# Output products of a two-layer linear-attention kernel: rounded parts replaced by plain float32, cut in pieces

## The chip, the cores and the metric

The kernel runs on one core of a Trainium2 chip. The metric is the device time of one execution in microseconds, the median of several runs. The core's engines each have a queue of their own: TensorE (PE in the profile, its weight loads PEld), VectorE (DVE), ScalarE (ACT), GpSimd (POOL) and SyncE (SP, which issues the DMAs here).

## The reference

The input x has 2048 rows of 640 columns, in float32. Two layers, each an attention part and a dense part, with the same weights in both:

```python
x = x + _A_ref(_layernorm(x, axis=-1), A_wqkv, A_w_phi, A_wo)
x = x + _B_ref(_layernorm(x, axis=-1), B_w1, B_b1, B_w2)
x = x + _A_ref(_layernorm(x, axis=-1), A_wqkv, A_w_phi, A_wo)
x = x + _B_ref(_layernorm(x, axis=-1), B_w1, B_b1, B_w2)
```

`_A_ref` forms queries, keys and values (32 heads of 20), maps queries and keys by a small matrix per head, takes the softmax of the result and of its negative as features, and does linear attention: `kv` and `z` are sums over all rows, and each row's output is a quotient of two products. The part that matters here is its last product, `o.reshape(B, S, D) @ wo`: 2048 x 640 by 640 x 640. `_B_ref` is a dense layer to 1536 columns, Mish, and a dense layer back to 640.

## The kernel before

Rows are worked on in 8 blocks (`NB`) of 256, each of two row tiles of 128 (`BT`). The 640 columns are 5 groups of 128 (`KD`) as an operand that is summed over, and two halves of 320 (`HC`) as an output.

Products that must be exact to float32 are made from rounded parts (`F32R`): an operand a is split into a high part (a rounded copy) and a low part (a less the high part), and one product becomes three: high by high, high by low, low by high. `project_half` (L352) does this for one half of one row tile: 5 x 3 = 15 matmuls into one PSUM tile. Some other products use plain float32 operands: `average` (L584, its matmuls at L594), the sums over keys (L432), and the folding of the feature matrices into the weights (`fold_phi`, L239, L250).

Each layer has three stages.

- `attend_first` runs over the blocks and makes queries, keys and values, and sums `kv` and `z` over all rows. After block 1 it also calls `load_o_weights` (L211), which reads the five row groups of `wo` through `make_five` (L199): raw rows are fetched into spare tiles, ScalarE makes the high part and GpSimd the low part (`make_parts`, L152 to L155).
- `attend_second` (L574) runs over the blocks again. `average` makes the attention output of one row tile in rows. `Transposed` (L279) turns two such tiles: TensorE transposes them into PSUM (L294), ScalarE copies the high part out (L299, recorded at its helper's line, L122), VectorE subtracts for the low part (L300). `Rows.half` (L621) then makes one half of one row tile of the output product, adds it to x (L624) and takes statistics of the sum (L625). In each block there are four such halves: r0's two go to two `one_tile`s, r1's two to one `mm_tile`. In between, the averages of the next block and its transposes are issued. Meanwhile the weights of the dense part are fetched and split (`fetches`, `makes`).
- `dense` does the two dense layers over the blocks, its matmuls at L703 and L745.

The order of instructions on TensorE and SyncE is written out by hand in `attend_second` (`tc.manual_schedule`). Elsewhere, and on the other engines, a planner orders the work by simulated times (`tc.block(schedule_with_timeline_sim=True)`), save where the code says what an instruction is to follow.

Of the kernel before, what the change touches and what calls it, by code (L numbers as in the profile page):

```python
# [8 lines left out]
F32 = mybir.dt.float32  # L9
F32R = mybir.dt.float32r  # L10
AF = mybir.ActivationFunctionType
# [5 lines left out]
P = 128  # L17
S = 2048
D = 640
# [3 lines left out]
KD = D // P  # L23
KF = F // P
BT = 2
BLK = BT * P
# [3 lines left out]
HC = D // 2  # L30
# [18 lines left out]
def kernel(  # L49
# [13 lines left out]
    nc = tc.nc  # L63
# [47 lines left out]
    x1_d = dram.tile([S, D], F32, name="x1_d")  # L111
# [40 lines left out]
    def make_parts(w, raw, ordered=False):  # L152
        for st, cs in raw:
            (act if ordered else nc.scalar.activation)(w[0][:, cs], st, AF.Copy)
            nc.gpsimd.tensor_tensor(w[1][:, cs], st, w[0][:, cs].bitcast(F32), op=ALU.subtract)  # L155
# [11 lines left out]
    def r2_pair(j):  # L167
        if j >= 10:
            w = r2_wide(j)
            return w[:, 0], w[:, 1]  # L170
        return tuple(wts.tile([P, D], F32R, tag=f"r2{s}{j}", name=f"r2{s}{j}") for s in "hl")
# [24 lines left out]
                nc.sync.dma_start(wp_d[1, s, k], kv_ws[k][s][:, :FW].bitcast(F32))  # L196
                nc.sync.dma_start(wp_d[0, s, k], q_ws[k][s][:, :FW].bitcast(F32))

    def make_five(j, rows):  # L199

        spares = five_spares(j)
        raws = [fetch_rows(rows(k), [spares[k]()]) for k in range(3)]
        yield
        for k in range(5):
            w = r2_pair(j + k)
            make_parts(w, raws[k])
            if k in (0, 1):
                raws.append(fetch_rows(rows(3 + k), [spares[3 + k]()]))
            yield w

    def load_o_weights():  # L211
        return list(make_five(KD, lambda k: wo[k * P:(k + 1) * P, :]))[1:]

    def w2_pair(f):

# [63 lines left out]
    class Transposed:  # L279


        def __init__(self, rows=None, cols=None):
            self.rows, self.cols, self.hs, self.ls = rows, cols, [], []

        def step(self):
            c0 = len(self.hs)
            n = min(2, KD - c0)
            if self.rows is None:
                ps = self.cols[c0 // 2]
            else:  # L290
                ps = one_tile().rearrange("p (c s) -> p c s", c=2)
                for c in range(n):
                    for t in range(BT):
                        nc.tensor.transpose(ps[:, c, t * P:(t + 1) * P],  # L294
                                            self.rows[t][:, (c0 + c) * P:(c0 + c + 1) * P], ident)
            nb = 8 if n == 2 else 4
            hi = work.tile([P, n, BLK], F32R, tag=f"xt{n}", name="xth", bufs=nb)
            lo = work.tile([P, n, BLK], F32R, tag=f"xt{n}", name="xtl", bufs=nb)
            act(hi, ps[:, :n], AF.Copy)  # L299
            nc.vector.tensor_tensor(lo, ps[:, :n], hi.bitcast(F32), op=ALU.subtract)  # L300
            for c in range(n):
                self.hs.append(hi[:, c, :])
                self.ls.append(lo[:, c, :])
# [48 lines left out]
    def project_half(ps, xts, t, ws, col, c, ks=range(KD), w=HC):  # L352
        sl = slice(t * P, (t + 1) * P)
        cs = slice(col + c * w, col + (c + 1) * w)
        for k in ks:
            h, l, wh, wl = xts.hs[k], xts.ls[k], ws[k][0][:, cs], ws[k][1][:, cs]
            for n, (a, r) in enumerate(((h, wh), (h, wl), (l, wh))):
                nc.tensor.matmul(ps[:, :w], a[:, sl], r, start=(k == 0 and n == 0),  # L358
                                 stop=(k == KD - 1 and n == 2))

    def both(ps, w=HC):

# [208 lines left out]
                mask[:r, :w].unsqueeze(1).unsqueeze(3).to_broadcast([r, q, w, DH + 1]), op=ALU.mult)  # L571
        yield

    def attend_second(x_src, x_dst, acc, fetches, makes, fetch_next, begin_next):  # L574
        kva, o_ws, loaded, rest = acc
        rows = {}
        div = [None]

        def tail():

            with tc.issue_after(div[0]):
                next(rest, None)

        def average(b, t):  # L584

            phs = loaded[b]
            po = mm_tile()
            for g in range(G):
                n = 120 if g < 10 else 80
                w = GW if g < 10 else 42  # L590
                c, j = divmod(g, 8)
                for q in range(2):
                    s0 = t * P + 64 * q
                    nc.tensor.matmul(  # L594
                        po[64 * q:64 * q + 64, c, GW * j:GW * j + w], phs[g][:n, s0:s0 + 64],
                        kvb[:n, g, :w], start=True, stop=True)
            o = row_tile()
            den = work.tile([P, H], F32, tag="r", name="den", bufs=2)
            pv = [po[:, c, :(DH + 1) * n].rearrange("p (h d) -> p h d", d=DH + 1)
                  for c, n in ((0, 24), (1, 8))]  # L600
            hh = (slice(0, 24), slice(24, H))
            for c in range(2):
                nc.vector.tensor_scalar_add(den[:, hh[c]], pv[c][:, :, DH], DEN_EPS)
            nc.vector.reciprocal(den, den)
            for c in range(2):
                n = hh[c].stop - hh[c].start
                ins = nc.vector.tensor_tensor(o.rearrange("p (h d) -> p h d", d=DH)[:, hh[c]], pv[c][:, :, :DH],
                                        den[:, hh[c]].unsqueeze(2).to_broadcast([P, n, DH]), op=ALU.mult)
                div[0] = ins.ins
            rows.setdefault(b, []).append(o)  # L610
            if t == BT - 1:
                del loaded[b]

        class Rows:


            def __init__(self, b, t):
                self.t, self.xt, self.ps = t, xs[b], None
                self.bn = work.tile([P, 2, 6], F32, tag="bn", name="bn", bufs=2)

            def half(self, c, ps):  # L621
                project_half(ps, cur, self.t, o_ws, 0, c)
                part = self.xt[:, self.t, c * HC:(c + 1) * HC]
                nc.vector.tensor_tensor(part, ps[:, :HC], part, op=ALU.add)  # L624
                nc.vector.bn_stats(self.bn[:, c], part)  # L625

            def mean(self):
                mv = work.tile([P, 2], F32, tag="mv", name="mv", bufs=3)
                nc.vector.bn_aggr(mv, self.bn)
                return mv  # L630

        with tc.manual_schedule(engines={mybir.EngineType.PE, mybir.EngineType.SP}):
            kv = finish_kv(kva)
            next(kv)
            next(rest)
            next(kv)
            loaded[1] = load(1)
            xs = {0: fetch(x_src, 0)}
            fetches[0]()
            next(rest)  # L640
            next(kv)
            next(rest)
            average(0, 0)
            average(0, 1)
            loaded[2] = load(2)
            average(1, 0)
            cur = Transposed(rows.pop(0)).all()
            average(1, 1)
            loaded[3] = load(3)
            for b in range(NB):  # L650
                if b == NB - 1:
                    ahead.all()
                elif b:
                    average(b + 1, 0)
                r0, r1 = Rows(b, 0), Rows(b, 1)
                r0.half(0, one_tile())
                if 0 < b < NB - 1:
                    average(b + 1, 1)
                tail()
                if b + 1 < NB:  # L660
                    xs[b + 1] = fetch(x_src, b + 1)
                if 0 < b and b + 3 < NB:
                    loaded[b + 3] = load(b + 3)
                if b == NB - 3:
                    fetch_next()
                r0.half(1, one_tile())
                mv0 = r0.mean()
                if b == NB - 2:
                    ahead = begin_next()
                py = mm_tile()  # L670
                r1.half(0, py[:, 0])
                if b + 1 < NB:
                    nxt = Transposed(rows.pop(b + 1)).all()
                r1.half(1, py[:, 1])
                norm_scale(b, [mv0, r1.mean()])
                xt = xs.pop(b)
                nc.sync.dma_start(row_block(x_dst, b), xt)
                makes[b]()
                if b + 1 < NB:
                    fetches[b + 1]()  # L680
                tail()
                if b < NB - 1:
                    cur = nxt
            for _ in rest:
                pass
        return ahead
# [134 lines left out]
    with tc.block(schedule_with_timeline_sim=True):  # L821
        src, first = x, None
        for layer in range(LAYERS):
# [35 lines left out]
            def begin_dense():  # L859
                return normed(0, x1t[0])  # L860

            begun = attend_second(src, x1_d, acc, [lambda s=s: fetch_step(*s) for s in steps],
                                  [lambda s=s: make_step(*s) for s in steps], fetch_dense, begin_dense)
            first = dense(x1_d, dst, w1s, w2s, [x1t[0], begun, None], last)
            src = dst
# [38 lines left out]
```

## Time and profile before

| | |
|---|---|
| median of 3 runs | 1397.88 us (1397.22 to 1398.19) |
| the profiled execution | 1397.5 us |
| its span, first to last instruction | 1395.7 us |
| mean granted clock of TensorE | 0.996 |
| PE busy | 1364.8 us (98%) |
| DVE busy | 1080.8 us (77%) |
| ACT busy | 592.4 us (42%) |
| POOL busy | 466.4 us (33%) |
| `attend_second` of layer one, first average to last half | 268.6 to 373.3 us |
| `attend_second` of layer two, the same | 944.5 to 1048.8 us |

A row of a group in the profile reads: line, engine, operation, output tile <- input tiles, shapes, count, then busy time and mean duration of one in ns, then the engine's idle time before them and what ended it. A row in order of time reads: start in us, duration in us, engine, line and the same names. A row of a stretch has its limits and length, then the busy time and number of instructions of PE, PEld, DVE, ACT and POOL, the granted clock, the DMA engines' share and GB/s. Matmuls overlap and their ends are modelled, so what one costs in a row of them is read from start to start.

### The profile page before, as it was taken

The numbers are of one execution on the slowest core, as the hardware profiler recorded it, in microseconds if no ns is written. First come the engines' busy times: TensorE is split into PE (matmuls) and PEld (weight loads), VectorE is DVE, ScalarE is ACT, GpSimd is POOL, SyncE is SP. The second block draws the span as 40 slices with busy tenths as digits, with TensorE's granted clock in tenths as the row PEclk, the third lists the DMA queues.
The fourth block names the chain that finished last, engine by engine and source line by source line (L and its number), as shares of the span: only waits on it lengthen the run. The fifth ranks groups of instructions, "written<-read, shape, count | busy, mean of one in ns | idle before, by whom it ended". The sixth has DMA issues, their size and how long they took to land. (4 is left out here: it accounts for less than half of the span.)

```text
span 1395.7 us, 30855 instructions
## 1 busy us (share of the span) xinstructions
PE 1364.8 (98%) x12866; PEld 1344.2 (96%) x12866; DVE 1080.8 (77%) x1814; ACT 592.4 (42%) x1039; POOL 466.4 (33%) x346
## 2 busy tenths in 40 slices
PE   7999999999999999999999999999999999999998
PEld 7989999899999999999999999999999999999998
DVE  5798888686688877788759988878667766777775
ACT  4444443321355454454454334332134544444443
POOL 1454544243442221222234454543344211211112
PEclk9999999999999999999999999999999999999999
DMA  8533423779534433444374333358965212333200
GB/s 312 166 60 77 75 41 70 204 224 317 194 89 95 100 82 60 102 114 95 103 258 85 78 72 70 58 126 253 273 246 172 76 29 68 95 96 95 59 37 20
DMA packets 350277, 169.03 MB, mean 121 GB/s; under 512 B 287097, under 2 KB 323689, under 8 KB 350137
## 3 DMA queue, kind: packets, MB, share of 16 engines
q1 hardware_dynamic: 350137, 167.06, 44.4%
q8 instruction: 101, 1.65, 0.5%
q14 instruction: 39, 0.32, 0.1%
HBM read 104.43 MB, written 62.59 MB: 120 GB/s over the span
## 5 line engine op out<-in xcount | busy, mean ns | idle before, releaser
L745 PE MATMUL mm<-r2h,ol 128*128 128x320 f32 x1280 | 305.3, 310 | 1.4 <-ACT ol L728 0.8
L729 POOL TENSOR_TENSOR ol<-big,ol 128x512 fp32r<-128x512 f32 (+1 forms) x98 | 130.1, 1329 | 456.2 <-ACT ol L728 390.9
L703 PE MATMUL one<-xtl,r1h 128*128 128x256 f32 x960 | 268.6, 280 | 2.0 <-DVE xtl L300 2.0
L703 PE MATMUL one<-xth,r1l 128*128 128x256 f32 x960 | 268.0, 279 | 0.0
L703 PE MATMUL one<-xth,r1h 128*128 128x256 f32 x960 | 266.5, 279 | 0.0
L745 PEld LDWEIGHTS mm<-r2h,ol 128*128 128x128 f32 x1280 | 219.1, 188 | 2.7 <-POOL ol L729 1.5
L745 PE MATMUL mm<-r2l,ol 128*128 128x320 f32 x640 | 197.3, 309 | 0.0
L358 PE MATMUL mm<-r1h,xth 128*128 128x304 f32 (+1 forms) x600 | 187.5, 313 | 6.6 <-ACT r L122 6.6
L358 PE MATMUL mm<-r1h,xtl 128*128 128x304 f32 (+1 forms) x600 | 184.7, 308 | 1.0 <-DVE xtl L300 1.0
L358 PE MATMUL mm<-r1l,xth 128*128 128x304 f32 (+1 forms) x600 | 184.4, 307 | 0.0
L703 PEld LDWEIGHTS one<-xtl,r1h 128*128 128x128 f32 x960 | 180.4, 188 | 2.7 <-DVE xtl L300 2.5
L703 PEld LDWEIGHTS one<-xth,r1l 128*128 128x128 f32 x960 | 180.4, 188 | 0.0
L703 PEld LDWEIGHTS one<-xth,r1h 128*128 128x128 f32 x960 | 179.9, 188 | 0.0
L718 DVE TENSOR_SCALAR big<-big 128x512 f32<-128x512 f32 (+1 forms) x98 | 55.9, 571 | 113.6 <-ACT big L716 113.5
L358 PE MATMUL mm<-r2h,xth 128*128 128x304 f32 (+1 forms) x460 | 142.2, 309 | 0.0
L358 PE MATMUL mm<-r2h,xtl 128*128 128x304 f32 (+1 forms) x460 | 140.4, 305 | 0.0
L358 PE MATMUL mm<-r2l,xth 128*128 128x304 f32 (+1 forms) x460 | 140.3, 305 | 0.0
L716 ACT ACTIVATE big<-one,b1s 128x256 f32<-128x256 f32 x192 | 80.8, 469 | 96.2 <-PE one L703 95.6
L358 PEld LDWEIGHTS mm<-r1h,xth 128*128 128x128 f32 x600 | 113.8, 190 | 8.1 <-ACT r L122 7.0
L720 ACT ACTIVATE big<-big,two 128x512 f32<-128x512 f32 (+1 forms) x98 | 70.3, 717 | 118.8 <-DVE big L719 116.2
L745 PEld LDWEIGHTS mm<-r2l,ol 128*128 128x128 f32 x640 | 120.2, 188 | 0.0
L399 POOL TENSOR_TENSOR r<-r,r 128x1280 f32<-128x1280 f32 x32 | 77.0, 2406 | 124.1 <-DVE r L398 108.7
(131 smaller groups left out, 3031.9 us busy)
## 6 DMA issues: line engine op xcount, KB each, us to landing
e_d<-r SPq DMA_DIRECT2D x128, 160.0 KB, 4.0
big<-e_d SPq DMA_DIRECT2D x32, 640.0 KB, 5.9
x_d<-xt SPq DMA_DIRECT2D x23, 640.0 KB, 3.9
xt<-x_d SPq DMA_DIRECT2D x22, 640.0 KB, 4.6
n_d<-xn SPq DMA_DIRECT2D x176, 80.0 KB, 2.3
xt<-in_x SPq DMA_DIRECT2D x16, 640.0 KB, 5.5
xn<-x_d SPq DMA_DIRECT2D x28, 320.0 KB, 4.1
v<-n_d SPq DMA_DIRECT2D x30, 256.0 KB, 3.1
```

The lines of the kernel that those rows point to most:

```text
L358: nc.tensor.matmul(ps[:, :w], a[:, sl], r, start=(k == 0 and n == 0), stop=(k == KD - 1 and n == 2))
L399: nc.gpsimd.tensor_tensor(eg, eg, r.unsqueeze(2).to_broadcast([P, 2 * H, DH]), op=ALU.mult)
L703: nc.tensor.matmul(ph[:, j, :], l, r, start=(n == 0), stop=(n == 3 * KD - 1))
L716: exps[0] = nc.scalar.activation(part(ta, 0)[:, j - js.start], ph[:, j, :], AF.Exp, bias=b1s[:, 2 * pr + j:2 * pr + j + 1]).ins
L718: nc.vector.tensor_scalar_min(e, e, E_CAP)
L720: nc.scalar.activation(r, n, AF.Ln, bias=two)
L729: nc.gpsimd.tensor_tensor(al[:, js], n, ah[:, js].bitcast(F32), op=ALU.subtract)
L745: nc.tensor.matmul(pys[t][:, c, :HC], l[:, j, sl], r, start=(f == 0 and n == 0), stop=(f == KF - 1 and n == 2))
```

## The change

The output product of attention takes whole operands in plain float32. `make_five` gets a flag: with it, ScalarE copies the raw rows of `wo` into a plain float32 tile, and no low part is made (the low tile is still allotted). `Transposed` gets a flag: with it, ScalarE copies the turned rows to a plain float32 tile, and VectorE's subtraction is left out. `project_whole` does one matmul per group of 128 summed columns and per piece of the output; the pieces are given by `cuts`. In layer one, each half of 320 is cut into 108, 106 and 106 columns. In layer two, row tile 0 is cut into 160 and 160, and row tile 1 is not cut.

```diff
-    def make_five(j, rows):
+    def make_five(j, rows, whole=False):
...
         for k in range(5):
-            w = r2_pair(j + k)
-            make_parts(w, raws[k])
+            if whole:
+                w = tuple(wts.tile([P, D], F32, tag=f"r2{s}{j + k}", name=f"r2{s}{j + k}") for s in "hl")
+                for st, cs in raws[k]:
+                    nc.scalar.activation(w[0][:, cs], st, AF.Copy)
+            else:
+                w = r2_pair(j + k)
+                make_parts(w, raws[k])
...
     def load_o_weights():
-        return list(make_five(KD, lambda k: wo[k * P:(k + 1) * P, :]))[1:]
+        return list(make_five(KD, lambda k: wo[k * P:(k + 1) * P, :], True))[1:]
...
             nb = 8 if n == 2 else 4
+            if self.whole:
+                hi = work.tile([P, n, BLK], F32, tag=f"xt{n}", name="xtw", bufs=nb)
+                act(hi, ps[:, :n], AF.Copy)
+                for c in range(n):
+                    self.hs.append(hi[:, c, :])
+                return
...
+    def project_whole(ps, xw, t, ws, c, cuts):
+
+        sl = slice(t * P, (t + 1) * P)
+        for k in range(KD):
+            for n, (c0, c1) in enumerate(zip(cuts, cuts[1:])):
+                nc.tensor.matmul(ps[:, c0:c1], xw.hs[k][:, sl], ws[k][0][:, c * HC + c0:c * HC + c1],
+                                 start=(k == 0 and n == 0), stop=(k == KD - 1), skip_group_check=True)
...
             def half(self, c, ps):
-                project_half(ps, cur, self.t, o_ws, 0, c)
+                cuts = (0, 108, 214, 320) if layer == 0 else ((0, 160, 320), (0, 320))[self.t]
+                project_whole(ps, cur, self.t, o_ws, c, cuts)
...
-            cur = Transposed(rows.pop(0)).all()
+            cur = Transposed(rows.pop(0), whole=True).all()
...
-                    nxt = Transposed(rows.pop(b + 1)).all()
+                    nxt = Transposed(rows.pop(b + 1), whole=True).all()
```

The rows that the dense part turns first (`begin_next`) keep their two parts, and so do all other products.

More of the change, by code (lines that the diff above doesn't have):

```diff
@@ L279, with __init__ @@
     class Transposed:
-        def __init__(self, rows=None, cols=None):
+        def __init__(self, rows=None, cols=None, whole=False):
             self.rows, self.cols, self.hs, self.ls = rows, cols, [], []
+            self.whole = whole
         def step(self):
@@ L572, in finish_kv, with attend_second @@
         yield
-    def attend_second(x_src, x_dst, acc, fetches, makes, fetch_next, begin_next):
+    def attend_second(layer, x_src, x_dst, acc, fetches, makes, fetch_next, begin_next):
         kva, o_ws, loaded, rest = acc
@@ L860, in begin_dense @@
                 return normed(0, x1t[0])
-            begun = attend_second(src, x1_d, acc, [lambda s=s: fetch_step(*s) for s in steps],
+            begun = attend_second(layer, src, x1_d, acc, [lambda s=s: fetch_step(*s) for s in steps],
                                   [lambda s=s: make_step(*s) for s in steps], fetch_dense, begin_dense)
```

## The prediction

> **What bounds the kernel now.** I read the page's first two parts, then the waits, then the stretches in which the changed products run, then the order of instructions inside one block of such a stretch.
>
> ```profile
> span 1395.7 us, 30855 instructions
> PE 1364.8 (98%) x12866; PEld 1344.2 (96%) x12866; DVE 1080.8 (77%) x1814; ACT 592.4 (42%) x1039; POOL 466.4 (33%) x346
> PEclk9999999999999999999999999999999999999999
> 268.60:366.44 97.84, 97.17 (x1215) 93.66 (x1215) 73.80 (x194) 24.47 (x41) 35.82 (x33) 1.00 0.78 246
> 944.47:1041.96 97.49, 96.81 (x1216) 93.31 (x1215) 74.11 (x197) 24.59 (x41) 35.81 (x33) 1.00 0.79 253
> PE mm L594 <- PE mm L594: 0.4, 1, 0.4
> PE one L358 <- DVE xtl L300: 0.2, 1, 0.2
> ```
>
> TensorE is busy for 98% of the span, and each of its 12866 matmul records has its own weight load record. The two rows of stretches (PE, PEld, DVE, ACT and POOL busy, then clock, DMA share, GB/s) are the two passes through the second half of attention, one per layer: 97.84 and 97.49 us, in which PE is idle 0.67 and 0.68 us, at a full clock. The last two rows are all the waits of PE that are listed inside them, one from each: 0.4 us behind its own averages and 0.2 us for a low part. Nothing else is late there. So whatever the change adds to PE's instructions in these stretches should come out at the end of the kernel, and what it takes off VectorE and GpSimd should not.
>
> **The products as they are.** One half (128 rows by 320 columns) is 5 x 3 = 15 products of rounded float32 parts. In the order of time (start, duration):
>
> ```profile
> 276.47 0.31 PE L358 MATMUL one<-r2l,xth 128*128 128x320 f32 x1
> ...
> 282.78 0.31 PE L358 MATMUL mm<-r2h,xtl 128*128 128x320 f32 x1
> 282.93 1.25 PE L294 MATMUL one<-ident,xn 128*128 128x128 f32 x10
> 267.20 0.46 PE L358 MATMUL one<-r2l,xth 128*128 128x304 f32 x1
> ...
> 268.22 0.46 PE L358 MATMUL one<-r2h,xtl 128*128 128x304 f32 x1
> 266.80:268.50 1.70, 1.70 (x8) 1.50 (x6) 1.05 (x4) 0.00 (x0) 0.00 (x0) 0.50 1.03 412
> ```
>
> Between 276.47 and 282.78 lie 43 steps from record to record (three halves less two records): 6.31 / 43 = 146.7 ns each, so a half takes 15 x 146.7 = 2.20 us. The row after them is the transposes of the next block's rows, which a later part uses. The last two steps of time are a piece at half the granted clock (0.50 in the last row): four steps in 1.02 us, 255 ns for 304 columns, 0.839 ns a column, which at the full clock is 0.4195. So 320 columns stream in 134.2 ns, and a rounded product has a fixed 12.5 ns on top.
>
> **The products as they will be.** Each half is 5 plain float32 products, cut into pieces. Layer one: three pieces (108, 106, 106). Layer two: two of 160 for row tile 0, one of 320 for row tile 1. With 8 blocks, 2 row tiles and 2 halves a layer, that is 32 halves in thirds, 16 in two pieces, 16 whole. The kernel has plain float32 products already: the averages (L594), the sums of keys and values (L432) and the folding of the feature weights (L250).
>
> ```profile
> L594 PE MATMUL mm<-kvb,big 120*64 120x63 f32 x1280 | 44.5, 225 | 0.9 <-PE mm L594 0.9
> L594 PE MATMUL mm<-kvb,ol 80*64 80x42 f32 x128 | 8.7, 212 | 0.0
> L432 PE MATMUL one<-big,v 128*21 128x40 f32 x2048 | 26.8, 205 | 0.0
> L250 PE MATMUL one<-big,raw x40: 261/275/421, 16.0 to 40.7; 120*128 120x114 f32 x40
> L703 PE MATMUL one<-xth,r1l 128*128 128x256 f32 x960 | 268.0, 279 | 0.0
> L745 PE MATMUL mm<-r2l,ol 128*128 128x320 f32 x640 | 197.3, 309 | 0.0
> 36.74 0.82 PE L250 MATMUL mm<-big,raw 120*128 120x114 f32 x6
> 37.39 0.83 PE L250 MATMUL one<-big,raw 120*128 120x114 f32 x6
> 38.06 0.83 PE L250 MATMUL mm<-big,raw 120*128 120x114 f32 x6
> 38.73 1.28 PE L250 MATMUL one<-big,raw 120*128 120x114 f32 x10
> 39.94 0.41 PE L250 MATMUL one<-big,r 40*128 40x38 f32 x2
> ```
>
> First, **the count**. An average issues 22 products, and there are 32 averages: 704, where the rows have 1280 + 128 = 1408. The sums of keys are 32 x 32 = 1024 products and 2048 records. So a plain product is two records, each with its own weight load. A half becomes 5 x 3 x 2 = 30, 5 x 2 x 2 = 20 or 5 x 2 = 10 records, in place of 15.
>
> Second, **the columns**. The duration of a plain record grows from 205 ns at 40 columns to 275 (median) at 114: 0.95 ns a column. That of a rounded one grows from 279 at 256 to 309 at 320: 0.47. So I take a plain record to stream at half the speed, 0.839 ns a column at full clock. The durations are ends that the profile models, so this is the weaker of the two readings; a rival below takes its opposite.
>
> Third, **the floor**. The three groups of six at 114 columns start 36.74 to 38.73: 1.99 us / 18 = 110.6 ns a record. Streaming 114 columns at 0.839 is 95.6, so something else holds the step, and the weight load of 128 columns, one to a record, is what is left. A piece of 108 streams in 90.6 and one of 106 in 88.9, so both should step at the same 110.6. The Trainium skill, "TensorE: Matmul & The Clock Gate", section LDWEIGHTS, prices a load at its columns over 1.2 GHz, 107 ns for 128, and its section on weight-path perf modes has no fast load for FP32; the trace is within 4 ns of that. By the page's figure a half in thirds would be 30 x 107 = 3.2 us.
>
> The **sum**, half by half:
> - Thirds: 30 x 110.6 = 3.32 us in place of 2.20, +1.12; 32 of them, +35.8 us. The lower bound is a piece at its streaming time with no load showing, 10 x 268.5 ns = 2.69 us a half (two records of 320 columns for each of 5 operands), +0.49 and +15.5 us in all; the upper is the last group above, 38.73 to 39.94 for ten, 121 ns: 3.63 us, +1.43, +45.8 us. I take 110.6, the row nearest in columns, in weights and in type.
> - Two pieces of 160: each streams 134.2 ns, above the floor. What is fixed on top is between 0 and the 12.5 of a rounded record; the loaded weights change as often, but the elements stream at half the rate. I take 6: 20 x 140.2 = 2.80 us, +0.60; 16 of them, +9.7 us (7.7 to 11.7).
> - Whole: 268.5 + 6 = 274.5; 10 of them 2.75 us, +0.54; 16 halves, +8.7 us (7.8 to 9.8).
>
> The same section's neighbour in the Trainium skill, Back-to-back issue gap, has 2.5 ns for what is fixed. The rounded products here show 12.5, so it does not hold for them; for plain ones no run yet says. By it the layer two terms would be +8.5 and +8.2.
>
> Together +54.2 us: PE's order is written by hand in this stretch, and every one of these records lies on it.
>
> **What is removed** is off the path:
>
> ```profile
> 296.05:309.17 13.12, 13.12 (x160) 12.63 (x158) 10.16 (x27) 2.74 (x4) 6.85 (x6) 1.00 1.01 284
> 296.05:309.17 13.12, 1.62 (x3) 1.00 1.01 284
> L155 POOL TENSOR_TENSOR r2l<-raw,r2h x24: 1562/1574/2115, 45.0 to 1079.9; 128x640 fp32r<-128x640 f32 x24
> ```
>
> The first row is one block, from its transposes to the next block's: PE 13.12 of 13.12 us, VectorE 10.16. The second is VectorE's three subtractions of the low parts (L300) in it, 1.62 us, which go away. VectorE had 3 us to spare and gets more; the wait of 0.2 us for a low part goes, since a block then needs only ScalarE's copy. The ScalarE copies stay, three a block, now to full float32. The low parts of the output weights go too: five GpSimd subtractions of 1.57 us a layer, in the first half of attention; neither wait of PE in the stretches that read them is on them. No transfer is added or moved: the raw rows come by the same five transfers into the same spare tiles, and the low tiles stay allotted. I cost all this at nothing. If that cover were gone (VectorE the bound of a block), the 1.62 us would be worth at most 16 x 1.62 = 26 us, but PE's full row excludes it. No wait is added: each reader of a half (L624) waits on its last piece as it did on its last product. The switches between averages and halves stay where they are. The planner that orders the engines outside the hand-written stretch works from simulated times and may order the dense part otherwise; PE's idle time between the two stretches and after them bounds a gain:
>
> ```profile
> 373.00:907.00 534.00, 528.16 (x4602) 523.93 (x4602) 438.58 (x662) 251.02 (x441) 178.91 (x126) 1.00 0.42 100
> 1048.00:1395.00 347.00, 341.57 (x2613) 340.29 (x2611) 242.57 (x401) 157.56 (x284) 75.99 (x59) 1.00 0.26 74
> ```
>
> It is 5.8 and 5.4 us. I take 0, with about 4 us either way.
>
> The profiled execution took 1397.5 us with its span of 1395.7, and the median of the runs is 1397.88. 1397.9 + 54 gives 1452.
>
> **The rivals.**
> A. A plain record streams a column as fast as a rounded one. Then thirds are still held at 110.6 (+35.8), two pieces too (20 x 110.6 = 2.21, +0.2 us in all), and whole records step at 146.7: 10 x 146.7 = 1.47, -0.73, 16 times -11.7. In all +24: 1422. For it: the step at 114 columns is held by the load and so says nothing on streaming. Against it: the slope of 0.95. 6%.
> B. The other side, faster: these products come out as one record and not two. Then 15 x 110.6 = 1.66 (-0.54 x 32 = -17.3), 10 x 146.7 (-11.7) and 5 x 281 = 1.41 (-0.79 x 16 = -12.7): -42, 1356. It decides as soon as a half in thirds has under 2200 / 110.6 = 19.9 records. For it: the transposes, also of float32, are one record each (ten in the row at 282.93, for 5 columns by 2 row tiles). Against it: all three kinds of real product in the rows are doubled. 3%.
> C. The granted clock drops while pieces wait for loads (they stream 90 of 110.6 ns). Layer one's halves would double: 32 x 3.32 = +106 more, 1558. For it: the clock of 0.50 at 266.8, after an idle of PE. Against: the groups at 36.74 and the averages run with loads as dense, under a clock of 9 tenths or more. 2%. The skill's same page, Part 1, ties the half clock to idle windows of about 3.4 us, which these stretches do not have.
> D. The loads are hidden or not repeated for pieces of one operand: thirds at +15.5 (above) to +28 (30 x 102 ns, with 12.5 fixed on each piece), in all +34 to +47, 1432 to 1445. Against: 12866 loads for 12866 matmuls, although neighbouring products of the dense part (L745) use the same weights. 8%.
>
> **How the numbers follow.** My case has 78%, A 6, B 3, C 2, D 8, and 3 for a planner's order that costs more than I allow. From my case's bounds: low, thirds at 107 with nothing fixed elsewhere, 1445; high, 121 and 12.5, 1465; the planner's few microseconds lie inside. The range reaches into D: 1441 to 1464. About 0.2%, 2.8 us, is what a measurement can tell from no change. Only B is faster: 0.03; within 0.2%: 0.01; slower: 0.96.
>
> **What would show it.** In the changed profile: 32 x 30 + 16 x 20 + 16 x 10 = 1440 matmul records of the output products in place of 64 x 15 = 960; a step of about 110 ns for widths 108 and 106, 140 for 160, 275 for 320; the first stretch longer by 36 us, the second by 18; PE's waits in them unchanged; VectorE less busy by 1.6 us a block. A step near 90 in thirds, or 147 for a whole record, would make me wrong; so would a new wait of PE in the two stretches.

## The result, and the profile after

The changed kernel takes 1447.71 us (median of four runs, 1446.24 to 1449.26) against 1398.04 us: slower by a ratio of 1.0352 (95% interval 1.0333 to 1.0371), 49.7 us. The profiled execution took 1449.26 us with a span of 1447.4, 51.7 us more than the profiled span before. From the page of the changed kernel:

```profile
span 1447.4 us, 31733 instructions
PE 1418.2 (98%) x13346; PEld 1384.9 (96%) x13346; DVE 1054.7 (73%) x1766; ACT 592.3 (41%) x1039; POOL 449.8 (31%) x336
```

TensorE is still busy for 98% of a longer span, with 480 records more, each with a weight load; VectorE lost 48 instructions and 26 us, GpSimd 10 and 17 us. Next the two stretches of `attend_second`, from the first average to the first matmul of the dense part. The first two rows are of the kernel before, the next two of the changed one; the last is all that TensorE waits for in the two of the changed kernel.

```profile
268.60:373.12 104.52, 103.84 (x1260) 100.34 (x1260) 78.11 (x205) 26.47 (x45) 40.80 (x38) 1.00 0.79 251
944.47:1048.64 104.17, 103.49 (x1261) 99.99 (x1260) 78.43 (x208) 26.72 (x45) 40.84 (x38) 1.00 0.80 259
266.94:407.38 140.44, 140.33 (x1725) 137.92 (x1725) 68.21 (x181) 27.08 (x45) 42.08 (x39) 0.99 0.61 192
980.52:1099.58 119.06, 118.63 (x1266) 102.79 (x1265) 67.77 (x184) 26.96 (x45) 40.90 (x38) 1.00 0.71 228
PE mm L614 <- PE mm L614: 0.4, 1, 0.4
```

Layer one's stretch grew by 35.9 us, layer two's by 14.9; together 50.8 of the 51.7. TensorE is idle for at most 0.7 us in each, before and after, so the loss is work and not waiting. (The last half of a layer is issued past the limit, behind the first matmuls of the dense part, so 31 of 32 halves lie in each row, and in the two stretches of the table of times before.) In layer one the number of matmul records grew by 465, 31 x 15; in layer two it stayed but for that last half, and yet it cost 15 us: there records became longer.

The records themselves, in order of time (start, then the time that the group takes):

```profile
299.90 3.51 PE L378 MATMUL mm<-r2h,xtw 128*128 128x108 f32 x30
303.25 1.26 PE L300 MATMUL one<-ident,xn 128*128 128x128 f32 x10
1020.77 2.98 PE L378 MATMUL one<-r2h,xtw 128*128 128x160 f32 x20
1023.59 2.85 PE L378 MATMUL mm<-r2h,xtw 128*128 128x320 f32 x10
1026.28 1.25 PE L300 MATMUL one<-ident,xn 128*128 128x128 f32 x10
```

From the start of one group to the start of the next, a half in thirds takes 3.35 us for 30 records, 111.7 ns each. A whole half takes 2.69 us for 10, 269 ns each. The half in two pieces takes 2.82 us for 20, with the change from the averages in it. A half of the kernel before takes 2.20 us.

### The profile page after: what moved, and what is told of

The parts are those of the page before. It is cut to its first block, busy times and chain, and to the rows that moved or that the text cites. A ratio compares the mean times of both kernels' runs of the same rounds, so it can differ in the third digit from the quotient of the medians.

```text
span 1447.4 us, 31733 instructions
## 1 busy us (share of the span) xinstructions
PE 1418.2 (98%) x13346; PEld 1384.9 (96%) x13346; DVE 1054.7 (73%) x1766; ACT 592.3 (41%) x1039; POOL 449.8 (31%) x336
## 5 line engine op out<-in xcount | busy, mean ns | idle before, releaser
L749 ACT ACTIVATE ol<-big 128x512 fp32r<-128x512 f32 (+1 forms) x98 | 61.0, 622 | 133.3 <-DVE big L748 133.2
L370 PEld LDWEIGHTS mm<-r1h,xtl 128*128 128x128 f32 x600 | 113.4, 189 | 0.3
L370 PEld LDWEIGHTS mm<-r1l,xth 128*128 128x128 f32 x600 | 113.5, 189 | 0.1
```

Source lines behind the costliest of these rows:

```text
L749: nc.scalar.activation(ah[:, js], n, AF.Copy)
```

## The experiments

Twelve kernels ran. Unless an edit is said to be on the kernel before, it is on the changed one. Times are medians, ratios are against runs of the kernel before on the same chip.

**Uncut (e1) and in two pieces everywhere (e2).**

```diff
-                cuts = (0, 108, 214, 320) if layer == 0 else ((0, 160, 320), (0, 320))[self.t]
+                cuts = (0, 320)          # e1
+                cuts = (0, 160, 320)     # e2
```

> All 64 halves as uncut plain products of 320 columns. Theory (a record costs the larger of its streaming time and the load of 128 weight columns): the step stays at the 269 ns that the changed kernel shows for 320 columns, a half takes 10 x 269 = 2.69 us against 2.20 of the rounded ones, 64 x 0.49 = +31 us on 1398: about 1429. Rival (what layer one loses is not the load but the stretch itself, such as its clock or its averages): the cut does not matter and layer one keeps its loss of 36 us, in all 1446.

> All 64 halves cut in two pieces of 160. Theory (streaming against load): 160 columns stream in 134 ns, above the load, so the step is 135.5 ns and a half takes 20 x 135.5 = 2.71 us: 64 x 0.51 = +33 us, 1430, within 2 us of the uncut kernel although it has twice the records. Rival (every record has a price of its own on top of its streaming, the 20 ns that pieces of 108 show): 20 x 155 = 3.1 us, +57 us, 1455.

Measured: 1426.19 us (1.0190, 1.0167 to 1.0212) and 1427.06 us (1.0199, 1.0177 to 1.0220). A half of e2 away from a change of work, in order of time:

```profile
295.81 2.88 PE L378 MATMUL mm<-r2h,xtw 128*128 128x160 f32 x20
298.53 1.25 PE L300 MATMUL one<-ident,xn 128*128 128x128 f32 x10
```

That is 20 records in 2.72 us, 136 ns each, and 10 records of 320 columns took 2.69. Twice as many records cost next to nothing at this width, where a piece streams for 134 ns, longer than the 112 ns at which the thirds step. The rival of e2, a fixed price of 20 ns on each record, is out. The two stretches of e1:

```profile
267.29:387.12 119.83, 119.83 (x1106) 90.72 (x1105) 67.47 (x181) 26.98 (x45) 40.73 (x38) 0.98 0.70 222
958.41:1078.02 119.61, 119.17 (x1106) 90.02 (x1105) 67.47 (x181) 26.72 (x45) 40.23 (x37) 0.99 0.70 223
```

They are 15.3 and 15.4 us longer than before, 30.7 together; the step has 31 x (2.69 - 2.20) = 15.2 for each. The medians differ by 26 only (the runs of the kernel before beside it had a median of 1400.04, and the profiled run of e1 was the longest of its four), and no run takes these 4 us apart. So the rival of e1 is out, since layer one's loss changes with the cut: thirds in place of whole halves cost 140.44 - 119.83 = 20.6 us of the 35.9, and plain float32 uncut the other 15.3.

**Layer one in quarters (e3).**

```diff
-                cuts = (0, 108, 214, 320) if layer == 0 else ...
+                cuts = (0, 80, 160, 240, 320) if layer == 0 else ...
```

> Layer one in four pieces of 80, layer two as changed. Theory (the load of 128 columns is a floor under every record): the step stays at 111 ns although 80 columns stream in 67; 40 x 111 = 4.44 us a half, 32 x 2.24 = +72, with layer two's 15 in all +87: 1485. Rival (streaming and a fixed 21 ns on each): the step is 88 ns, 3.52 us a half, +42 and 15: 1455.

Measured: 1482.04 us (1.0596, 1.0571 to 1.0620).

```profile
300.16 4.69 PE L378 MATMUL one<-r2h,xtw 128*128 128x80 f32 x40
304.69 4.52 PE L378 MATMUL mm<-r2h,xtw 128*128 128x80 f32 x39
```

40 records from 300.16 to 304.69, 113 ns each with a change from the averages in it. The second row is cut by its window; the whole half of 40 starts at 304.69 and the transposes behind it at 309.16, which is 111.7 ns each. Pieces of 80 step no faster than pieces of 108: a floor, and not a price on top of the streaming.

**Rounded products in pieces: thirds in layer one (e4), two pieces everywhere (e10).** Both edit the kernel before.

```diff
-                nc.tensor.matmul(ps[:, :w], a[:, sl], r, start=(k == 0 and n == 0),
-                                 stop=(k == KD - 1 and n == 2))
+                cs_ = (0, w) if cuts is None else cuts
+                for i, (c0, c1) in enumerate(zip(cs_, cs_[1:])):
+                    nc.tensor.matmul(ps[:, c0:c1], a[:, sl], r[:, c0:c1], start=(k == 0 and n == 0 and i == 0),
+                                     stop=(k == KD - 1 and n == 2), skip_group_check=cuts is not None)
...
-                project_half(ps, cur, self.t, o_ws, 0, c)
+                project_half(ps, cur, self.t, o_ws, 0, c, cuts=(0, 108, 214, 320) if layer == 0 else None)   # e4
+                project_half(ps, cur, self.t, o_ws, 0, c, cuts=(0, 160, 320))   # e10
```

> The kernel before, with layer one's rounded products cut at 108 and 214: 45 records a half in place of 15, each streaming 45 ns. Theory (the load is the same floor whatever the type): the step is 111 ns, 45 x 111 = 5.0 us a half, 32 x 2.8 = +90: 1487. Rival (the floor of 111 belongs to plain float32; a rounded piece costs its streaming and 12.5 ns): 45 x 57 = 2.58 us, +12: 1410.

> The kernel before with all rounded halves cut in two pieces of 160: 30 records a half, each streaming 67 ns under a load of 111. Theory (the larger of the two counts): a step of 111 ns, 30 x 111 = 3.33 us a half, 64 x 1.13 = +72 us, 1470, and so 43 us slower than plain float32 in the same pieces (1427). Rival (a rounded piece costs 67 + 12.5 = 80 ns): 2.39 us, +12, 1410.

Measured: e4 1486.64 us (1.0626, 1.0606 to 1.0645), e10 1470.08 us (1.0508, 1.0494 to 1.0523). Two rows of e4, 36 records apart, and two of e10, 26 apart:

```profile
291.10 0.50 PE L360 MATMUL mm<-r2h,xtl 128*128 128x108 f32 x3
...
295.12 0.50 PE L360 MATMUL mm<-r2h,xtl 128*128 128x108 f32 x3
```

```profile
292.37 0.39 PE L360 MATMUL one<-r2l,xth 128*128 128x160 f32 x2
...
295.27 0.39 PE L360 MATMUL one<-r2h,xtl 128*128 128x160 f32 x2
```

4.02 us / 36 = 111.7 ns and 2.90 / 26 = 111.5 ns. The floor is the same for rounded products, whose 160 columns stream in 67 ns. So here the cheaper form changes with the width: at 320 columns, three rounded records of 146.7 (440 ns) beat two plain ones of 269 (538); at 160, three at the floor (335) lose to two of 136 (272). e10 is 43 us slower than e2.

**Half the weights to load, plain thirds (e7).** In layer one the output product is made for the first 64 rows of each row tile; the other 64 get none.

```diff
-        sl = slice(t * P, (t + 1) * P)
+        sl = slice(t * P, t * P + m)
...
-                nc.tensor.matmul(ps[:, c0:c1], xw.hs[k][:, sl], ws[k][0][:, c * HC + c0:c * HC + c1],
+                nc.tensor.matmul(ps[:m, c0:c1], xw.hs[k][:, sl], ws[k][0][:, c * HC + c0:c * HC + c1],
...
+                m = 64 if layer == 0 else P
...
-                nc.vector.tensor_tensor(part, ps[:, :HC], part, op=ALU.add)
+                nc.vector.tensor_tensor(part[:m], ps[:m, :HC], part[:m], op=ALU.add)
```

> The changed kernel with the output product in layer one made for the first 64 rows of each row tile only (the other 64 get none), so each record loads 64 weight columns in place of 128 and streams the same 108 or 106. Theory (the load is the floor): it falls to about 55 ns, the streaming of 90 ns decides, the step is about 91, a half in thirds 2.73 us in place of 3.34: 32 x 0.61 = 20 us less than the changed kernel, 1428. Rival (a floor of 111 ns under any plain record of this size, whatever it loads): 1448, no change.

Measured: 1426.87 us (1.0202, 1.0188 to 1.0216). A half, in order of time, the group of its loads, and a group of full loads in layer two of the same run:

```profile
292.69 2.91 PE L378 MATMUL mm<-r2h,xtw 128*64 128x108 f32 x30
L378 PEld LDWEIGHTS mm<-r2h,xtw 128*64 128x64 f32 x480 | 44.4, 136 | 1.3 <-DVE bn L647 1.0 <-issue 0.2
L378 PEld LDWEIGHTS one<-r2h,xtw 128*128 128x128 f32 x320 | 43.8, 190 | 0.6
```

With 0.25 us for the last record, 29 steps take 2.66 us, 91.7 ns each. Same columns, same number of records, half the loaded weights: the step falls from 111.7 to about what 108 columns stream in (90.6). A load record falls from 190 to 136 ns, 54 ns for 64 columns, which at that rate would be 108 for 128, near the floor. So the floor is the weight load. The edit also halves the rows of the output that a record writes, and no run changes these alone; in e8 below, the same halving takes 2 to 3 ns off a step that is above the floor.

**Half the weights to load, rounded products (e8), on the kernel before,** with the same edit in `project_half`, layer one.

> The kernel before with the rounded output product in layer one made for the first 64 rows of each row tile only: 64 weight columns a record, 320 columns streamed. A plain record of 320 or 160 columns has about 1 ns on top of its streaming, a rounded one 12.5. Theory (the load beside it takes reads from a record that streams at full rate): half the load, half of it, a step of 140 ns: 32 x 15 x 6.3 = 3 us less, 1395. Rival (it has nothing to do with the load): 146.7 ns, 1398.

Measured: 1398.16 us (0.9998, 0.9989 to 1.0006).

```profile
287.08 0.30 PE L358 MATMUL one<-r2l,xth 128*64 128x320 f32 x1
...
288.95 0.31 PE L358 MATMUL one<-r2h,xtl 128*64 128x320 f32 x1
```

13 steps in 1.87 us, 143.8 ns; a later half, whose second record starts at 322.06 and last at 323.94, has 144.6. That is 2 to 3 of the 6.3 that the theory wanted, and nothing in the total that is clear of its interval. Where the rest of the rounded records' 12.5 ns comes from stays open.

**No subtraction of the low part (e5), on the kernel before.**

```diff
-            lo = work.tile([P, n, BLK], F32R, tag=f"xt{n}", name="xtl", bufs=nb)
+            lo = hi
+            if self.sub:
+                lo = work.tile([P, n, BLK], F32R, tag=f"xt{n}", name="xtl", bufs=nb)
...
-            nc.vector.tensor_tensor(lo, ps[:, :n], hi.bitcast(F32), op=ALU.subtract)
+            if self.sub:
+                nc.vector.tensor_tensor(lo, ps[:, :n], hi.bitcast(F32), op=ALU.subtract)
```

> The kernel before without the subtraction that makes the low part of the turned rows in the second half of attention (48 on VectorE in all); the products read the high part in its place, so TensorE issues the same. Theory (TensorE sets the pace, VectorE's 1.62 us a block are hidden): no change, 1398 within 1 us. Rival (the subtractions are part of the pace and the change was given some of them back): up to 26 us less, 1372.

Measured: 1396.66 us (0.9991, 0.9980 to 1.0002). The work that the change takes off VectorE was hidden: by the interval, taking it away gains at most 0.2% of the time, 2.8 us, and the 26 us of the rival are out.

**Two of three products (e6), and that without the subtraction (e9), on the kernel before.**

```diff
-            for n, (a, r) in enumerate(((h, wh), (h, wl), (l, wh))):
+            for n, (a, r) in enumerate(((h, wh), (h, wl), (l, wh))[:m]):     # m = 2 in the output product
```

> The kernel before with two of the three rounded products (low by high left out of the output product): 10 records a half in place of 15. Theory (each step of TensorE in this stretch counts in full): 64 x 5 x 146.7 = 46.9 us less, 1351. Rival (VectorE is next: a block of TensorE would be 13.12 - 2.93 = 10.19 us, and VectorE's block is 10.16): TensorE begins to wait for VectorE in the stretch and a good part is lost, 1355 to 1375.

> Two of the three rounded products, as in the run that gained 25 us of 47, and besides without the subtraction that makes the low part, which nothing reads then (low by high is left out of the output product). Theory (in that run VectorE had become the pace of a block, and its 1.62 us of subtraction, hidden before, were on the path): VectorE's block falls from 10.16 to 8.5 us, under TensorE's 10.19, the waits for it go and the whole 46.9 us come out: 1351. Rival (what held TensorE there is the order of VectorE's other work, the sums and the quotients, and not its load): the waits stay, 1365 to 1373.

Measured: e6 1373.27 us (0.9814, 0.9796 to 0.9832); e9 1371.79 us (0.9805, 0.9792 to 0.9819). With low by high left out, both are faster than the kernel before, e6 by 25 us and e9 by 27; but 22 and 20 us of the expected 47 do not come. The theory of e9 fell, and its rival's number came out. e9's two stretches, and in them one wait of the transfer queue (layer one) and one of VectorE (layer two):

```profile
267.92:358.82 90.90, 84.38 (x1106) 78.79 (x1105) 63.62 (x181) 27.05 (x44) 39.32 (x37) 0.98 0.90 284
934.13:1025.16 91.03, 84.92 (x1106) 78.75 (x1105) 63.82 (x184) 26.59 (x44) 38.96 (x36) 0.98 0.90 288
SPq L408 <- DMA x_d<-xt: 21.4, 5, 7.3
DVE xt L628 <- DMA xt<-x_d: 11.5, 5, 3.4
```

TensorE is idle for 6.5 of 90.90 us, and VectorE, which its waits name, is busy for 63.62 only: its load is not the pace. The granted clock of 0.98 is worth an estimated 1.8 us more (0.02 of 90.90). The DMA engines are busy for 0.90 of the stretch, where it was 0.79 before. In layer one the queue waits 21.4 us for rows of x to be written out before it may fetch others into their tile, and in layer two VectorE waits 11.5 us for x to come.

**A third tile for x (e11), and no writes of x in layer two (e12), both on e9.**

```diff
-        return work.tile([P, BT, D], F32, tag="x", name="xt", bufs=2)
+        return work.tile([P, BT, D], F32, tag="x", name="xt", bufs=3)      # e11; xt2, xt1: 6 and 3 tiles
...
-                nc.sync.dma_start(row_block(x_dst, b), xt)
+                if layer == 0:                                             # e12
+                    nc.sync.dma_start(row_block(x_dst, b), xt)
```

> The kernel of two products without the subtraction, with three tiles for x in place of two; the room comes from the turned rows, six and three tiles in place of eight and four, which can cost time in the other stages, so the length of the two stretches is what is read. In the run before, each stretch took 91 us where TensorE's work is 104.5 - 23.5 = 81. Theory (the fetch of the next block's x waits for its tile's old rows to be written out, up to 7 us, and holds the queue of transfers behind it): with a third tile the stretches fall to 81 to 84 us. Rival (the transfers themselves are the pace, the DMA engines being busy 0.9 of the stretch): they stay at 89 to 91.

> The kernel of two products without the subtraction, and in layer two without the writes of x after attention (the dense part of layer two reads the rows of layer one in their place). It takes 640 KB of transfers from each block of layer two and the wait of the fetch with them. If transfers, by their wait or by their volume, are what TensorE waits for: layer two's stretch falls from 91 to 81 to 84 us, layer one's stays at 91, the total falls by 7 to 10 from 1372. Rival (VectorE or the order of work holds TensorE): both stretches stay at 91.

Measured: e11 1380.79 us (0.9865, 0.9849 to 0.9880), e12 1365.03 us (0.9745, 0.9728 to 0.9761). The stretches, first two rows e11, next two e12; the last two are waits of the queue in e11's layer one:

```profile
273.25:363.27 90.02, 84.25 (x1105) 78.75 (x1105) 64.05 (x183) 27.04 (x44) 39.21 (x37) 0.98 0.89 290
941.95:1033.30 91.35, 85.55 (x1106) 80.20 (x1105) 63.64 (x180) 26.47 (x44) 38.90 (x36) 0.96 0.87 279
268.20:360.41 92.21, 84.91 (x1106) 78.93 (x1105) 63.44 (x181) 26.99 (x44) 39.00 (x36) 0.98 0.88 278
933.33:1018.00 84.67, 82.19 (x1105) 77.67 (x1105) 63.99 (x178) 26.59 (x44) 39.66 (x37) 1.00 0.84 260
SPq L408 <- DMA x_d<-xt: 3.5, 2, 2.6
SPq L681 <- DVE xt L628: 19.1, 4, 7.6
```

A tile more did not shorten either stretch, and e11 as a whole is 9 us slower than e9, with fewer tiles for the turned rows. The wait for the tile fell from 21.4 to 3.5 us, but the queue then waits longer for VectorE at the writes of x, 19.1 us where e9 has 12.9: the fetches behind them are still held. Taking the writes away did shorten layer two, from 91.0 to 84.7 us, and left layer one as it was. So in layer two of a kernel shortened this much, the transfers of x cost TensorE 6.4 us. Whether by their volume or by writes that hold the one queue stays open, since e12 takes away both. For layer one it is an inference from the like share of 0.90; no wait of VectorE for x is listed there. In the kernel before, 104 us of TensorE's work cover this.

## Why the prediction was right

**The bound.** TensorE's work in the two stretches was to come out at the end in full. It did: 50.8 of 51.7 us lie there, and e5 shows the work removed from VectorE was worth nothing that can be told from no change. (VectorE's busy time fell by 9.9 and 10.7 us in the two stretches, 1.2 and 1.3 a block, where 1.6 was named; it bears on nothing here.) What I had not seen is how near the next limit lies in the other direction: of the 47 us that e6 and e9 take off TensorE, 22 and 20 do not come out.

**The count.** 1440 records in place of 960, two to a product: as forecast.

**The floor** (thirds, 30 x 110.6 ns, +35.8 us): the step is 111.7 ns and the stretch grew by 35.9. That these two agree to 0.1 us is partly luck: the forecast was for 32 halves, for which the step gives 32 x (3.35 - 2.20) = 36.8, and the stretch holds 31. That the load of 128 columns is the floor was inferred from one row at 114 columns; e3, e4 and e10 show it at 80, 108 and 160 columns and for both types, and e7 takes it away. So rival D (loads hidden or not repeated) is out. The figure in the Trainium skill, "TensorE: Matmul & The Clock Gate", section LDWEIGHTS, 107 ns for 128 columns, is 4% low here.

**The columns.** That a plain record streams at half the speed was right: 269 ns is twice the 134.2 of 320 columns. Rival A, 147 ns for a whole record, is out. But the row it was argued from does not show it. I took the rise of the mean duration from 205 ns at 40 columns to 275 at 114 for streaming. The groups of the changed kernel, and then one of e4, whose rounded pieces stream in 45 ns:

```profile
L378 PE MATMUL mm<-r2h,xtw 128*128 128x106 f32 x320 | 48.7, 274 | 0.0
L378 PE MATMUL one<-r2h,xtw 128*128 128x160 f32 x320 | 47.1, 303 | 0.0
L378 PE MATMUL mm<-r2h,xtw 128*128 128x320 f32 x160 | 45.7, 432 | 0.0
L360 PE MATMUL mm<-r2h,xtl 128*128 128x106 f32 x160 | 30.9, 274 | 0.0
```

A rounded piece of 106 shows the same 274 ns as a plain one: at the floor, the duration tells nothing of streaming. Only from 160 to 320 columns, above the floor, is the slope a measure: 129 ns / 160 = 0.81 a column. So half speed was right, but by luck in so far as the row that I read it from does not show it; 6% for rival A was low for what I knew.

**What is fixed on top of streaming** is the term that was mis-sized. I took 6 ns between bounds of 0 and 12.5; e2's 136 and the 269 leave 1 to 2 over the streaming of 134.2 and 268.5. Layer two was to cost 18.4 us. By the measured steps it is 16 x (2.72 - 2.20) + 16 x (2.69 - 2.20) = 8.3 + 7.8 = 16.1, of which 15.6 lie within the limits of the stretch, and that grew by 14.9; the 0.7 us still missing no run took apart. The 12.5 ns belong to the rounded records alone. The 2.5 ns of the Trainium skill, "TensorE: Matmul & The Clock Gate", section Back-to-back issue gap, fits the plain records and not the rounded ones: with 320 columns passed twice at the page's 2.4 GHz it gives an estimated 269 ns, and the trace has 269.

**The sum.** 1452 was forecast; the profiled span grew by 51.7 against 54.2, and the medians by 49.7. With their last halves, layer one came out 1.3 us above its term (37.1 for 35.8) and layer two 3.0 below (15.4 for 18.4), so the two errors partly cancel. The medians differ from the profiled pair by 2 us, about what single runs of one kernel differ by here (1446.24 to 1449.26).

**The planner** left the rest alone, or nearly: outside the two stretches the span grew by 0.9 us. The two last halves past their limits are 1.15 + 0.49 = 1.64 of work added there, so all else became 0.7 us shorter, well inside the 4 us that I allowed.

## What to carry to other kernels

Price a matmul by records: with 128 loaded columns, each cost here the larger of its streaming time (and 1 to 2 ns for plain records, 12.5 for rounded ones) and a load of about 112 ns. So count records, not columns, once a piece streams in less than that, and read it from start to start, since a record's duration stops falling there (274 ns at 106 columns and at 80 in e3). This was measured for products that fill the rows of the output, or its first 64. It does not hold for the averages, whose records load 64 columns and write the two halves of the rows in turn: 1280 of them keep TensorE busy for 44.5 us, 35 ns each, where 63 columns alone would stream for 53. On these numbers a plain float32 product (two records at half speed) is dearer than three rounded ones where an output is wide and cheaper where all of them sit at the load, as at 160 columns. Before cutting a full engine's work, look at the share of the next resource. At a DMA share of 0.79 before, 20 of 47 us did not come out, and in layer two 6.4 of them are shown to be the transfers of x.

## What the runs showed of the hardware that was not expected

Rounded records of 320 columns step at 146.7 ns, 12.5 over their streaming, while plain ones, which take twice as long to stream as many columns, have 1 to 2; with half the weights to load a rounded one steps at 143.8 to 144.6. No run explains the rest.

The four runs of the changed kernel differ as the clock that they were granted: it took 1449.26 and 1448.78 us at a mean of 0.994 and 0.995, and 1446.64 and 1446.24 at 0.998 and 0.997.
